# A new step plan, a new order of the setup and ten table columns on GpSimd, in a spectral-filter and maxout kernel

## The chip, the cores and the metric

The kernel runs on one core of one Trainium2 chip. The metric is the device time of one execution in microseconds (us). The span of a profiled execution is some 1.8 us shorter than the time that the device reports for it; spans are compared with spans, and times with times.

The profiled execution of the kernel before is not one of its two timed runs (528.76 and 528.07). It took 530.12 us with a span of 528.4, so that the span is only by chance equal to the median time of 528.41.

## The reference, cut to what matters

```python
B, seq, dim = 8, 3072, 256                     # 24,576 tokens
X = np.fft.rfft(x, axis=1)                     # along the sequence, per batch and channel
Y = X * (filt_r + 1j * filt_i)[None]           # one filter for all batches
y = np.fft.irfft(Y, n=3072, axis=1).astype(np.float32).reshape(24576, 256)
h1, h2 = y @ w1, y @ w2                        # 256 -> 1024
out = np.maximum(h1, h2) @ w_out               # 1024 -> 256
```

## The kernel before

The sequence of 3072 is split into 128 x 24, and each transform is done as two stages of matrix products with a product by the filter between them. The kernel uses max(h1, h2) = relu(h1 - h2) + h2, so the second half of the network needs one product with w1 - w2 (tile `ph`), a relu, and two products that add up in `po`.

The setup (the first 48 us) builds the sine tables, spreads the filter from the loaded rows over the partitions ("spreads", `expand_f`: products `pf`, copied into `F`), and sends batch 0 through all stages without a trip through memory (S1, T1, S2, S3, T2). Its order is written out by hand, since TensorE, ScalarE and VectorE take turns in it:

```python
    order = (1, 2, 3, 4, 5, 0, 6, 7)
    expand_f(1, 0, S)            # spread of group 1, real part, copied by ScalarE
    expand_f(2, 0, V)
    first_s1(0, S)
    expand_f(3, 0, V)
    sines_u(0)
    first_s1(1, S)
    # ... (cut: the rest, which the diff below shows)
    first_s1(5, S, 2)
    expand_f(6, 0, V)
    first_t1(1, V)
    first_t1(2, V)
    expand_f(1, 1, S)            # imaginary spreads from here on
```

After it comes the main loop: 48 output tiles of eight steps. In each step TensorE makes one `ph` of its own tile and two or three parts of `po` of the tile before. The transforms of the later batches are hung into steps by a plan:

```python
    def load_p(b, c):            # one x tile of batch b: two loads
        # ...
        for m in range(2):
            nc.sync.dma_start(out=xb[b, c][64 * m:64 * m + 64], in_=...)

    def fold_x(b, c):            # sums and differences of its halves, on Pool
        # ...
        for i, op in enumerate((OP.add, OP.subtract)):
            G.tensor_tensor(xb[b, c][:, i], xf[:, 0], xf[:, 1], op)

    def f1_read(b):              # eight reads of the first stage's result, from memory
        # ...
                    nc.sync.dma_start(out=bt[b][64 * blk:64 * blk + 48, t0:t0 + 8],
                                      in_=src[blk][:, e, 8 * h:8 * h + 8])

    def z_read(b, h):            # one read of half of the filtered spectrum
        # ...
        nc.sync.dma_start(out=zr[b][64 * h:64 * h + 64], in_=zd[b]...)

    def gen_f2(b):               # nine units: filter batch b, and first stage of b + 1
        # ...
        units = (2, 3, 4, 5, 6, 7) if b == 1 else (0, 1, 3, 4, 6, 7)
        for j, g in enumerate((4, 5, 6, 7, 2, 3, 1, 0)):
            if b + 1 < B and j in units:
                f1_half(b + 1, (3, 4, 5, 0, 1, 2)[units.index(j)] if b == 1 else units.index(j))
            # ... products px of bt, product with F on VectorE (pq), products pz of the group before,
            # ... copied by ScalarE (zt); every second group stores zd
            yield
```

```python
    def plan_x(n, steps, lag=12):
        for c, s_ in enumerate(steps):
            plan(s_, load_p, n, c)
            plan(s_ + lag, fold_x, n, c)
    # ...
    plan(5, f1_read, 1)
    plan_f2(1, spaced(15, 2.4, 9), 28, 36)      # nine units from step 15; z_read at 28 and 36
    # ... (cut: batch 2's x)
    plan(36, f1_read, 2)
    plan_x(3, spaced(24, 3, 6))                 # x of batch 3
    plan_f2(2, spaced(60, 2.5, 9), 74, 81)
    plan(83, f1_read, 3)
    plan_x(4, spaced(64, 3.5, 6))
    plan_f2(3, spaced(104, 3, 9), 121, 129)
    plan(130, f1_read, 4)
    plan_x(5, spaced(108, 3.5, 6))
    plan_f2(4, spaced(150, 3.3, 9), 168, 178)
```

The x loads, the reads of `bt` and `zr`, and the stores of `zd` are all issued by SyncE, one after the other. And from batch 2 on, the unit of F2(n) that comes first already needs a folded x tile of batch n + 1, because `f1_half(b + 1, ...)` is called ahead of `px`.

## Time and profile before

| | before |
|---|---|
| time, median of 2 runs | 528.41 us (528.07 to 528.76) |
| TensorE busy | 510.4 us, 97% of the span |
| start to first `ph` (the setup) | 48.2 us |
| first `ph` to the start of tile 7 (both stalls) | 78.3 us |
| half clock inside the loop | 3.41 us from 68.66 and 6.83 us from 113.03 |

The page, the waits and the table by stage are shown and read in the prediction. One more view is needed for the setup: VectorE's timeline just before its first copy of a spread (columns: start in us, busy us of the group, engine, line, operation, output and input, shape, number).

```profile
8.77 0.96 DVE L275 TENSOR_TENSOR uu<-uu 128x768 f32<-128x768 f32 x1
9.76 0.56 DVE L276 TENSOR_SCALAR uu<-uu 128x768 int32<-128x768 int32 x1
...
11.25 0.27 DVE L283 TENSOR_SCALAR uu<-uu,col 128x1 f32<-128x1 f32 x1
11.44 3.07 DVE L141 CAST F<-pf 128x512 bf16<-128x512 f32 x5
```

The cut lines are five of the ten column operations, 0.15 to 0.21 us each; they end at 11.2, and the operation on `ny` (L283) and the casts follow at once. VectorE is never idle here: what is taken off it ahead of the casts should bring them forward.

### The profile page before, as it was taken

To read this page: it belongs to the slowest core of one execution; us is meant where nothing else is said; L and a number is where in the kernel's file an instruction comes from. 1 tells how busy PE (TensorE), PEld (TensorE's weight loads), DVE (VectorE), ACT (ScalarE), POOL (GpSimd) and SP (SyncE) were. 2 spreads that over 40 slices of the span, in tenths; PEclk is the share of its full clock that TensorE was granted. 3 is DMA by queue.
4 is the path that set the end of the run, shared out by engine and by line. 5 is a ranking of instruction groups with operands and counts; after the bars stand their busy time and mean duration, and the time that the engine had idled before them with its cause. 6 is when DMAs were issued, how large, how long until landed. Compare 5 with 4: busy or idle time off the path is not lost.

```text
span 528.4 us, 12607 instructions
## 1 busy us (share of the span) xinstructions
PE 510.4 (97%) x5282; PEld 347.4 (66%) x5282; DVE 322.7 (61%) x438; ACT 336.6 (64%) x598; POOL 147.9 (28%) x168
## 2 busy tenths in 40 slices
PE   8999999969999999999999999999999999999997
PEld 3556656636667766676666666676766666677775
DVE  8987568423874476546784588546873588534442
ACT  7786659624886578856765576746775456545542
POOL 6684423352127302550055101830000000000000
PEclk9999989979999999999999999999999999999999
DMA  7994897989688979987898959996466935341212
GB/s 145 281 197 105 198 244 219 291 163 180 212 229 251 203 194 289 268 178 176 223 242 222 191 152 258 288 173 167 137 175 147 183 110 139 104 128 41 81 59 102
DMA packets 74093, 97.03 MB, mean 184 GB/s; under 512 B 5106, under 2 KB 49780, under 8 KB 73044
## 3 DMA queue, kind: packets, MB, share of 16 engines
q1 hardware_dynamic: 63012, 63.72, 53.5%
q0 software_dynamic: 11024, 32.51, 20.0%
q8 instruction: 41, 0.67, 0.6%
q14 instruction: 16, 0.13, 0.1%
HBM read 54.79 MB, written 47.19 MB: 193 GB/s over the span
## 4 chain that ended last, share of the span: by engine, by line
PE 86%; DMA 6%; DVE 3%; ACT 3%; issue 1%; SPq 0%; ACTq 0%
PE ph L610 31%; PE po L635 30%; PE po L630 7%; PE pz L447 4%; PE py L580 4%; DMA zd<-zt 3%; PE px L469 3%; PE pa L410 2%; DMA zr<-zd 1%; ACT F L514 1%; DMA bt<-ad 1%; PE pz L548 1%; DMA ad<-at 1%; PE pf L131 1%; PE pt L505 1%
## 5 line engine op out<-in xcount | busy, mean ns | idle before, releaser
L615 ACT ACTIVATE gt<-ph 128x512 bf16<-128x512 f32 x308 | 181.9, 602 | 127.2 <-PE ph L610 125.9
L635 PE MATMUL po<-Wo,gt 128*128 128x256 bf16 x1536 | 230.9, 273 | 0.0
L635 PEld LDWEIGHTS <-gt 128*128 128x128 bf16 x1536 | 150.8, 98 | 58.5 <-issue 1.0
L474 DVE TENSOR_TENSOR pq<-px,F 120x1024 bf16<-120x1024 f32 x112 | 131.8, 1219 | 30.8 <-PE px L469 30.5
L637 DVE COPY ot<-po 128x512 f32<-128x512 f32 x96 | 66.2, 690 | 104.8 <-PE po L635 104.5
L642 POOL DMA_DIRECT2D out_dram<-ot x47 | 25.7, 546 | 324.0 <-DVE ot L637 299.7
L402 POOL TENSOR_TENSOR xd<-xf 128x512 bf16<-128x512 f32 x72 | 89.1, 1267 | 38.8 <-DMA xf<-in_x_dram 30.9
L610 PEld LDWEIGHTS <-Wd 128*128 128x128 bf16 x768 | 71.0, 98 | 21.5 <-issue 13.0
L451 ACT ACTIVATE zt<-pz 112x512 bf16<-112x512 f32 x112 | 60.9, 601 | 18.7 <-PE pz L447 17.3
L613 DVE TENSOR_SCALAR gt<-ph 128x512 bf16<-128x512 f32 x76 | 52.2, 686 | 30.8 <-PE ph L610 24.9
L413 ACT ACTIVATE at<-pa 128x512 bf16<-128x512 f32 x72 | 39.1, 594 | 15.1 <-PE pa L410 14.5
L580 PE MATMUL py<-G,zr 128*128 128x128 bf16 x376 | 29.6, 221 | 5.2 <-DMA zr<-zd 4.7
L580 PEld LDWEIGHTS <-zr 128*128 128x128 bf16 x376 | 25.0, 99 | 8.0 <-issue 6.9
L447 PE MATMUL pz<-pq,VP 56*64 56x256 bf16 x448 | 28.8, 273 | 0.0
L447 PE MATMUL pz<-pq,VQ 56*64 56x256 bf16 x448 | 28.3, 271 | 0.0
L469 PE MATMUL px<-bt,U 48*64 48x256 bf16 x448 | 23.0, 276 | 1.8 <-DMA bt<-ad 1.8
L469 PEld LDWEIGHTS <-U 48*64 48x64 bf16 x448 | 11.6, 107 | 10.1 <-issue 5.4
L530 DVE TENSOR_TENSOR pq<-px,F 120x1024 bf16<-120x1024 f32 x11 | 13.2, 1221 | 3.5 <-ACT F L514 1.9
L447 PEld LDWEIGHTS <-VP 56*64 56x64 bf16 x448 | 13.6, 106 | 1.8 <-issue 1.7
L410 PE MATMUL pa<-xd,C 64*64 64x512 bf16 x144 | 14.8, 400 | 0.0
L514 ACT ACTIVATE F<-pf 128x1024 bf16<-128x1024 f32 x10 | 10.1, 1030 | 6.4 <-PE pf L134 6.4
L447 PEld LDWEIGHTS <-VQ 56*64 56x64 bf16 x448 | 13.4, 107 | 0.1
(389 smaller groups left out, 609.6 us busy)
## 6 DMA issues: line engine op xcount, KB each, us to landing
out_dram<-ot POOLq DMA_DIRECT2D x47, 512.0 KB, 5.0
xf<-in_x_dram SPq DMA_DIRECT2D x72, 256.0 KB
ad<-at SPq DMA_DIRECT2D x42, 256.0 KB
bt<-ad SPq DMA_DIRECT2D x56, 192.0 KB
zd<-zt SPq DMA_DIRECT2D x56, 192.0 KB
zr<-zd SPq DMA_DIRECT2D x14, 768.0 KB
xb<-in_x_dram POOLq DMA_DIRECT2D x12, 256.0 KB, 10.4
wf<-in_moe_w_dram POOLq DMA_DIRECT2D x2, 1024.0 KB, 10.4
```

Source lines behind the costliest of these rows:

```text
L402: G.tensor_tensor(xb[b, c][:, i], xf[:, 0], xf[:, 1], op)
L413: S.activation(at[:, 2 * m:2 * m + 2], pa[m], AF.Copy)
L447: TE.matmul(pz[c][64 * k:64 * k + 64, i], W[64 * c:64 * c + 56, 2 * g + i, k], pq[k][64 * c:64 * c + 56, ri, i], start=(ri == 0), stop=(ri ...
L451: S.activation(zt[0:ROWS, c, o:o + 2], pz[c][0:ROWS], AF.Copy)
L469: TE.matmul(px[k][64 * c:64 * c + 64, i], U[64 * k:64 * k + 48, 4 * g + 2 * i + c], bt_[64 * k:64 * k + 48, t_], start=True, stop=True)
L474: V.tensor_tensor(pq[k][0:FROWS], px[k][0:FROWS].rearrange("p (o i) d -> p o i d", o=1).to_broadcast([FROWS, 2, 2, D]), F[0:FROWS, :, k, 2 ...
L580: TE.matmul(py[:, n], zr[b][:, 4 * i + n, 128 * dc:128 * dc + 128], G1, start=True, stop=True)
L610: TE.matmul(ph, Wd[:, dc, 128 * j:128 * j + 128], y_[:, dc].rearrange("p a b -> p (a b)"), start=(dc == 0), stop=(dc == 1))
L613: V.tensor_scalar(gt[tt][:, j], ph, 0.0, None, OP.max)
L615: S.activation(gt[tt][:, j], ph, AF.Relu)
L635: TE.matmul(p_, g_[:, jj, 128 * n:128 * n + 128], Wo[:, jj], start=False, stop=(jj == 7))
L637: V.tensor_copy(ot[tt][:, n - 1:n + 1], po[tt])
```

## The change

Its intent: take away the two waits of TensorE for memory in batch 1 and 2, by moving units and by moving x loads out of the way of a store; start the first filter load earlier; take ten small operations off VectorE; and get the spreads, which unblock the first groups, ahead of S1.

```diff
+    load_f(0)                                   # ahead of three iotas
     tq = init.tile([128, 2, T], FP32)
 ...
-    load_f(0)
 ...
-    load_f(1)                                   # moved behind tables_u
 ...
-        V.tensor_scalar(mk[:, 0:1], ab, -TWO_PI, TWO_PI, OP.mult, OP.add)
-        V.tensor_tensor(mx, pb, ab, OP.add)
 ...                                             # ten such lines: V becomes G
+        G.tensor_scalar(mk[:, 0:1], ab, -TWO_PI, TWO_PI, OP.mult, OP.add)
+        G.tensor_tensor(mx, pb, ab, OP.add)
+        G.tensor_scalar(mk[:, 1:2], mx, TWO_PI, None, OP.mult)
+        G.tensor_scalar(mh, mk, 0.25, None, OP.mult)
+        G.tensor_scalar(mm, mk, -1.0, None, OP.mult)
+        G.tensor_scalar(t2, pn, 0.5, None, OP.mult)
+        G.tensor_scalar(na, t2, RND, RND, OP.add, OP.subtract)
+        G.tensor_tensor(t2, t2, na, OP.subtract)
+        G.tensor_scalar(t2, t2, t2, 2.0, OP.mult, OP.mult)
+        G.tensor_tensor(t2, t2, nb, OP.mult)
 ...
-        V.tensor_scalar(ny, ny, pb, t1, OP.mult, OP.add)
+        V.tensor_scalar(ny, ny, pb, t2, OP.mult, OP.add)
 ...
     expand_f(1, 0, S)
     expand_f(2, 0, V)
-    first_s1(0, S)
     expand_f(3, 0, V)
     sines_u(0)
-    first_s1(1, S)
+    first_s1(0, S)
     expand_f(4, 0, V)
     sines_u(1)
+    first_s1(1, S)
+    expand_f(5, 0, V)
     first_s1(2, S)
-    expand_f(5, 0, V)
+    expand_f(0, 0, V)
+    sines_u(2)
     first_s1(3, S)
-    sines_u(2)
-    expand_f(0, 0, V)
+    expand_f(6, 0, V)                           # real spread of group 6 during S1
     first_s1(4, V, 2)
 ...
     first_s1(5, S, 2)
-    expand_f(6, 0, V)
+    expand_f(1, 1, S)                           # imaginary spreads ahead of and around T1
     first_t1(1, V)
     first_t1(2, V)
-    expand_f(1, 1, S)
-    expand_f(7, 0, S)
+    expand_f(2, 1, S)
 ...                                             # spread 7 and the fix of F's first column: later;
                                                 # not shown: two copies of C1 on Pool, moved behind the tables
-    plan_f2(1, spaced(15, 2.4, 9), 28, 36)
+    plan_f2(1, spaced(17, 2.25, 9), 28, 36)
 ...
-    plan(36, f1_read, 2)
-    plan_x(3, spaced(24, 3, 6))
-    plan_f2(2, spaced(60, 2.5, 9), 74, 81)
-    plan(83, f1_read, 3)
-    plan_x(4, spaced(64, 3.5, 6))
+    plan(37, f1_read, 2)
+    plan_x(3, spaced(38, 3, 6))
+    plan_f2(2, spaced(58, 2.4, 9), 70, 78)
+    plan(80, f1_read, 3)
+    plan_x(4, spaced(83, 3, 6))
     plan_f2(3, spaced(104, 3, 9), 121, 129)
     plan(130, f1_read, 4)
-    plan_x(5, spaced(108, 3.5, 6))
+    plan_x(5, spaced(132, 3, 6))
     plan_f2(4, spaced(150, 3.3, 9), 168, 178)
```

More of the change, by code (lines that the diff above doesn't have):

```diff
@@ L233, in tables_u @@
         col = init.tile([128, 16], FP32)
-        pb, p6, pa_, pn, n2s, nb, ab, mx, na, t1 = [col[:, i:i + 1] for i in range(10)]
-        mk = col[:, 10:12]
-        mh = col[:, 12:14]
-        mm = col[:, 14:16]
+        pb, p6, pa_, pn, n2s, nb, ab, ah, t1 = [col[:, i:i + 1] for i in range(9)]
         m5 = init.tile([128, 2], FP32)
@@ L245, in tables_u @@
         V.tensor_tensor(ab, pa_, nb, OP.mult)
-        V.tensor_scalar(mk[:, 0:1], ab, -TWO_PI, TWO_PI, OP.mult, OP.add)
-        V.tensor_tensor(mx, pb, ab, OP.add)
-        V.tensor_scalar(mk[:, 1:2], mx, TWO_PI, None, OP.mult)
-        V.tensor_scalar(mh, mk, 0.25, None, OP.mult)
-        V.tensor_scalar(mm, mk, -1.0, None, OP.mult)
+        gc = init.tile([128, 10], FP32)
+        mk, mh, mm = gc[:, 0:2], gc[:, 2:4], gc[:, 4:6]
+        mx, t2, na = gc[:, 6:7], gc[:, 7:8], gc[:, 8:9]
+        G.tensor_scalar(mk[:, 0:1], ab, -TWO_PI, TWO_PI, OP.mult, OP.add)
[8 more added lines that the diff above has]
+        G.tensor_tensor(t2, t2, nb, OP.mult)
         V.tensor_scalar(m5[:, 0:1], pb, 0.5, None, OP.mult)
@@ L271, in tables_u @@
                             ub[:, dr].rearrange("p (o j) -> p o j", o=1).to_broadcast([128, T, J]), OP.add)
-        V.tensor_scalar(ab, ab, 0.25, None, OP.mult)
-        V.tensor_scalar(w[:, 0, 1], w[:, 0, 1], ab, None, OP.subtract)
+        V.tensor_scalar(ah, ab, 0.25, None, OP.mult)
+        V.tensor_scalar(w[:, 0, 1], w[:, 0, 1], ah, None, OP.subtract)
         V.tensor_scalar(a, w, RND, RND, OP.add, OP.subtract)
@@ L276, in tables_u @@
         V.tensor_scalar(a.bitcast(mybir.dt.int32), w.bitcast(mybir.dt.int32), 0x7FFFFFFF, None, OP.bitwise_and)
-        V.tensor_scalar(t1, pn, 0.5, None, OP.mult)
-        V.tensor_scalar(na, t1, RND, RND, OP.add, OP.subtract)
-        V.tensor_tensor(t1, t1, na, OP.subtract)
-        V.tensor_scalar(t1, t1, t1, 2.0, OP.mult, OP.mult)
-        V.tensor_tensor(t1, t1, nb, OP.mult)
         ny = a[:, 0, 0, 0:1]
-        V.tensor_scalar(ny, ny, pb, t1, OP.mult, OP.add)
+        V.tensor_scalar(ny, ny, pb, t2, OP.mult, OP.add)
         return uu, (mk, mh, mm), t1
@@ L652 @@
     table_c()
-    for e in range(2):
-        G.tensor_copy(C1.rearrange("p (e x u w) -> p e x u w", e=2, x=8, u=2)[:, e],
-                      Cz.rearrange("p (x u e w) -> p e x u w", x=8, u=2, e=2)[:, e])
     Zt = late.tile([128, 2, 128, N2], BF16, tag="l0", name="Zt")
@@ L662 @@
     uu, mk, t1 = tables_u()
-    done = []
+    load_f(1)
+    for e in range(2):
+        G.tensor_copy(C1.rearrange("p (e x u w) -> p e x u w", e=2, x=8, u=2)[:, e],
+                      Cz.rearrange("p (x u e w) -> p e x u w", x=8, u=2, e=2)[:, e])
     wf = load_w()
@@ L700 @@
             tables_pe()
-            expand_f(2, 1, S)
         if n < 6:
-            expand_f((0, 3, 4, 5, 6, 7)[n], 1, S)
+            expand_f((3, 4, 5, 0, 6, 7)[n], 1, S)
         if n < 2:
             load_x(1, 4 + n)
-        if n == 2:
-            fix_f()
         if n in (1, 3):
             tables_q(n // 2, S)
+        if n == 3:
+            fix_f()
+        if n == 4:
+            expand_f(7, 0, S)
         if n in (4, 6):
@@ L792, in in_f2 @@
     def in_f2(step):
-        return 0 <= step < 6 or 15 <= step < 36 or 60 <= step < 82 or 104 <= step < 130
+        return 0 <= step < 6 or 17 <= step < 36 or 58 <= step < 79 or 104 <= step < 130
     for tt in range(6 * B + 1):
```

## The prediction

> **What bounds the kernel now.** I began with the page's head: the busy shares, the 40-slice table and the chain that ended last.
>
> ```profile
> PE 510.4 (97%) x5282; PEld 347.4 (66%) x5282; DVE 322.7 (61%) x438; ACT 336.6 (64%) x598; POOL 147.9 (28%) x168
> PEclk9999989979999999999999999999999999999999
> PE 86%; DMA 6%; DVE 3%; ACT 3%; issue 1%; SPq 0%; ACTq 0%
> ```
>
> TensorE (PE) is the bound: 97% busy and 86% of the chain. But the chain also holds 6% of DMA, and the granted clock dips in slices 6 and 9, at about 66-79 and 106-119 us. PE therefore loses time in a few places. I asked the view of waits for PE alone, first from 66 us to the end and then from 120 us to the end; what the second still shows is the rest.
>
> ```profile
> PE py L580 <- DMA zr<-zd: 4.7, 1, 4.7
> PE px L469 <- DMA bt<-ad: 1.8, 2, 1.0
> ...
> PE ph L610 <- DVE pq L474: 0.7, 2, 0.3
> ```
>
> Columns: who waited for whom, us in total, times, longest. Past 120 us PE waits for 0.7 us in 408 us: what the new step plan does to batches 3 to 7 can win nothing there. The two DMA waits, at 65-67 and 110-115 us, are what the plan can win. The table by stage gives their price (columns: window, its length, busy us with instruction counts of PE, PEld, DVE, ACT, POOL, then granted clock, DMA share, GB/s).
>
> ```profile
> 60.00:65.00 5.00, 5.00 (x43) 3.59 (x41) 1.98 (x3) 2.88 (x5) 0.00 (x0) 1.00 0.84 133
> 65.00:70.00 5.00, 3.21 (x22) 1.77 (x22) 3.02 (x3) 1.17 (x3) 0.63 (x1) 0.87 1.25 158
> 70.00:75.00 5.00, 5.00 (x69) 3.01 (x67) 3.23 (x5) 2.80 (x7) 0.38 (x1) 0.79 1.09 267
> 110.00:115.00 5.00, 0.64 (x6) 0.33 (x4) 0.69 (x1) 0.60 (x1) 2.32 (x3) 0.80 1.01 198
> 115.00:120.00 5.00, 4.36 (x20) 2.51 (x21) 0.91 (x2) 1.20 (x2) 0.00 (x0) 0.51 1.28 160
> ```
>
> After each wait the clock falls to half: the raw clock records give 0.50 from 68.66 to 72.07 us (3.41 us) and from 113.03 to 119.86 us (6.83 us), and 1.00 in all the rest but the last 0.9 us. The chain in order of time says what the long wait was for:
>
> ```profile
> 92.02 9.81 DMA zd<-zt
> 101.83 0.02 issue
> 101.84 7.01 DMA zd<-zt
> 108.85 0.02 SPq L429
> 108.88 0.03 issue
> 108.91 6.34 DMA zr<-zd
> ```
>
> The last spectrum tiles of batch 1 left ScalarE at 98.5 us (timeline). The SyncE queue issued their store only at 100.23, because it stood 3.8 us in the issue of two x loads of batch 3; the store then took 7.0 us beside those loads, and the read back 6.3.
>
> **What the Trainium skill says.** "TensorE: Matmul & The Clock Gate", Part 1, gives a free-running activity window of 3413 ns after which an idle PE falls to half clock. The trace agrees: 3.41 and 6.83 us are one and two such windows. "DMA: Bandwidth & Descriptors", Issuing engines are not separate DMA queues, says that transfers of all issuing engines interleave on the same 16 engines. The trace agrees: stores zd of later batches with no load beside them go from issue to the issue of their read in 3.8-4.1 us (281.06 to 285.11, 340.13 to 344.13), against 7-10 us here. "SBUF — State Buffer", Who interferes with whom, says that VectorE in a two-port mode, or with two SBUF inputs, can block GpSimd; the trace before has no small Pool arithmetic in the table stage, so this is untested, and it counts as a risk for the ten moved columns.
>
> **Part 1, the step plan.** A step of the main loop without other work costs 0.98 us: eight steps from 102.66 to 110.5 us.
> - Start of F2(1), step 15 to 17. The first px starts at 64.95 and its last matmuls wait for bt until 67.34; step 16 begins at 67.57. A px alone costs 0.34 us, so the loss is 67.57-64.95-0.34 = 2.28 us. Two steps later it starts at 64.95+2x0.98 = 66.91 in the same frame and still waits about 0.3. Gain 1.95. The half clock then stretched 68.56 to 71.92 us (3.36 us) over work that costs 0.98+0.34+0.44 = 1.76 at full clock: 1.6 us, which goes too if the wait does. **Sum 3.5 us.**
> - The x loads of batch 3, steps 24-39 to 38-53: behind the read of zr. Call T0 the end of step 35, where the last zd tiles are now made (before: step 34). ScalarE empties them by T0+1.2; the store, free of loads, takes 4.05, so the read is issued at T0+5.3 and lands 6.3 later: T0+11.6. PE needs it after 12 steps and one s4: 12x0.98+0.45 = T0+12.2. The wait of 4.74 us should shrink to 0-0.5; I take 0.2. The half clock after it cost 2.0 us (116.66 to 120.39 for two steps worth 1.96, and 0.25 on py). **Sum 6.5 us.**
> - The denser units (2.25 steps apart, not 2.4; 2.4, not 2.5): ScalarE was without idle from 86.3 to 96.3 us, and with 14 relus of 0.56, six units of 2.18 and two y of 0.6 it needs 22.1 us for 14 steps in which PE needs about 21.8. **Cost 0.3 us.**
> - Will the later loads starve F2(2), now at step 58? They are issued behind bt(2), from about T0+14 on; the first lands near T0+18, is folded by T0+20.5, and step 58 is T0+23.5. Hidden, as are the moves of batches 4 and 5.
>
> **Part 2, the setup** (first 48.2 us, where PE waits little but PE, ScalarE and VectorE take turns).
> - The first filter load is issued ahead of three iotas of 0.37, 0.34 and 0.18 us: at 1.22, not 1.97. PE waits for it until 8.85, with its warm-up matmuls ending at 7.97. It and the six x tiles behind it (one each 1.25 us, DMA saturated) land 0.75 earlier.
> - Ten column operations of 0.15-0.21 us leave VectorE: 0.6 us ahead of the large table, 0.9 us behind it. VectorE's first cast, at 11.44, can start near 9.95 if Pool has its columns done by then.
> - VectorE gets the casts of group 6 (1.2 us) ahead of the last S1 copy, not behind it; ScalarE's chain of spreads, sines and S1 copies (9.51 to 18.72, nearly without idle) starts 0.75 earlier, but sines_u(2) now leaves a gap of some 0.7 us in it. T1 thus starts at 18.4-18.9, hardly earlier than 18.78. What wins is after it: two ScalarE copies of F (1.03 us each) fewer stand between the first groups. I reckon pq of group 2 at 24.3 (25.33 before) and of group 3 at 26.2 (27.65).
> - Later Pool gives some of it back: fix_f waits for F0's patch at 32.8, and spread 7 comes back on ScalarE at n=4. First ph at 47.4 instead of 48.2. **Gain 0.8 us.**
>
> **Sum:** 528.4 - 3.5 - 6.5 + 0.3 - 0.8 = 517.9; I put 518.0.
>
> **Rivals.**
> - *The zd store is hidden no better.* Its half of the plan moved one step later, and an output store of 512 KB still runs beside it. For: the read alone takes 6.3 us and leaves 0.6 us of slack. Against: the uncontended stores of 4.0 us. If the store takes 6 us, the wait is 1.5 us and may bring back the half clock: 520-521.
> - *ScalarE becomes the bound in the denser batch.* For: 10 us without idle at the old spacing. Against: those units still cost PE 1.10 us each, its own work. It would cost 1-2 us: 519-520.
> - *The setup gets slower.* Pool's ten columns wait on VectorE's port, and the tables end late. Against: they have 7.1 to 9.9 us for some 2 us of work. It would cost up to 1 us: 519-520.
> - *Everything is won*: both waits gone entirely and the setup ahead by 1.4: 516.
>
> **Range and chances.** The sum lies on the line of 2% (517.8), so the chances split. Errors point both ways: a full win gives 516, each rival alone 519-521. I give 515.6 to 521.2 eight times in ten; faster by over 2% 0.46, within 2% 0.53, slower 0.01.
>
> **What the profile after should show.** Clock 1.00 from start to end but for the last us; PE's wait for zr under 0.6 us and for bt under 0.5; a zd store of batch 1 in 4-5 us with no x load between it and the store before; the x loads of batch 3 in one run behind bt(2); first pf near 8.1 us, first VectorE cast near 10, T1 near 18.6, first ph near 47.4; the same PE busy time past 120 us. The prediction is wrong if a half-clock window stays, if PE waits for xd or bt at the start of F2(2), or if the setup's 0.8 us turns negative.

## The result

The changed kernel takes 534.50 us (median of 2 runs, 534.33 to 534.66) against 528.41. The ratio of after to before is 1.0115, with a 95% interval of 1.0071 to 1.0158. Here and below a ratio is the mean time of one kernel's fast runs over that of the other's of the same rounds, so it is not quite the ratio of the medians. 534.50 lies outside the predicted range of 515.6 to 521.2. The times differ by 6.1 us and the spans of the two profiled executions by 4.1, since the profiled one of before was slower than the timed ones.

The lines of the page of the kernel after that answer to those shown of before:

```profile
PE 507.1 (95%) x5204; PEld 348.1 (65%) x5282; DVE 321.9 (60%) x429; ACT 336.6 (63%) x597; POOL 151.9 (29%) x178
PEclk9999999999999999997999999999999999999999
PE 79%; DMA 7%; SPq 4%; DVE 3%; POOL 2%; issue 2%; ACT 2%; POOLq 0%; ACTq 0%
```

The page shows 3.3 us less of busy time on TensorE, but this is not a saving: the profile of after lacks 78 matmul records, 75 of them of `ph`, and shows 3.1 us of idle time without a cause ahead of `po` in their place (0.0 before). With these added it is 510.2 us against 510.4, in a span that is 4.1 us longer, so TensorE waited more. The two dips of the clock in slices 6 and 9 are gone, as intended. There is a new one in slice 19 (about 239 to 253 us), in a place where the kernel before had no wait at all. The chain has lost 7 points of TensorE and gained 4 of SPq, SyncE's sequencer. TensorE's waits past the setup (who waited for whom, us in total, times, longest):

```profile
PE pa L409 <- POOL xd L401: 6.4, 4, 2.9
PE ph L609 <- DVE pq L473: 0.9, 3, 0.3
PE px L468 <- DMA bt<-ad: 0.5, 1, 0.5
```

The wait for `zr` (4.7 us) is gone and that for `bt` fell from 1.8 to 0.5. In their place stands a wait for `xd`, an x tile folded by Pool: two of its four times in 118 to 136 us, where F2(2) starts, and two in 225 to 264 us, where F2(4) starts. The table by stage (columns as in the prediction) shows the place of the old stall and that of the new one:

```profile
110.00:115.00 5.00, 4.39 (x36) 3.00 (x34) 1.98 (x3) 2.16 (x5) 0.53 (x1) 1.00 1.26 163
115.00:120.00 5.00, 5.00 (x43) 3.68 (x41) 2.10 (x4) 2.97 (x5) 0.00 (x0) 1.00 1.17 246
...
240.00:245.00 5.00, 1.27 (x13) 0.63 (x13) 0.00 (x0) 0.46 (x1) 2.48 (x2) 0.89 1.06 306
245.00:250.00 5.00, 5.00 (x26) 2.50 (x20) 2.95 (x3) 2.28 (x4) 4.14 (x4) 0.50 1.07 233
```

At 110 to 120 us TensorE now works at full clock; before, it was busy for 0.64 us of the first five and then at a clock of 0.51. But at 240 to 245 us it is busy for 1.27 of 5 us, and the next five run at half clock: the raw record says 6.83 us of it.

What all of this is worth can be summed without a remainder, because every output tile has a first `ph`. The table below gives the length of seven stretches of the span, from the start of one tile to that of another, for both kernels and for the runs of the next section.

| run | setup, to tile 0 | tiles 0-6 | 7-11 | 12-17 | 18-19 | 20-46 | 47 and end | span |
|---|---|---|---|---|---|---|---|---|
| before | 48.2 | 78.3 | 50.5 | 59.1 | 21.1 | 255.1 | 16.0 | 528.4 |
| after | 50.3 | 69.4 | 54.2 | 59.1 | 28.1 | 255.1 | 16.3 | 532.5 |
| e1 plan only | 48.4 | 69.6 | 54.6 | 59.1 | 26.4 | 255.1 | 16.0 | 529.2 |
| e2 setup only | 50.3 | 75.4 | 50.8 | 59.1 | 21.1 | 255.1 | 16.3 | 528.1 |
| e3 x loads back | 50.3 | 78.5 | 51.0 | 61.4 | 21.1 | 255.1 | 16.3 | 533.7 |
| e4 x loads of 4, 5 back | 50.3 | 68.8 | 55.9 | 60.8 | 21.1 | 255.1 | 16.3 | 528.4 |
| e11 two x tiles first | 50.3 | 68.8 | 52.6 | 59.1 | 27.0 | 255.1 | 16.3 | 529.1 |
| e8 x of batch 3 split | 48.3 | 69.1 | 51.0 | 59.1 | 21.1 | 255.1 | 16.0 | 519.8 |
| e12 e8 and setup mended | 47.5 | 69.3 | 51.5 | 59.1 | 21.1 | 255.1 | 16.3 | 519.9 |

From before to after: setup +2.1, tiles 0-6 -8.9, tiles 7-11 +3.7, tiles 18-19 +7.0, end +0.3, rest 0; the sum is +4.2, and the spans differ by 4.1. The stalls of before were won almost as predicted, in this pair of executions; part of the 8.9 is half clock (10.24 us of it before, none here after), which differs from execution to execution. They came back later, and the setup lost.

**Where the new wait comes from.** SyncE's queue in the kernel after, from the last `zd` store of batch 1 on (start, time in issue, queue, operation, number):

```profile
99.13 1.05 SPq L455 DMA_DIRECT2D zd<-zt  x2
103.33 0.47 SPq L428 DMA_DIRECT2D zr<-zd  x1
103.91 8.46 SPq L422 DMA_DIRECT2D bt<-ad  x8
112.48 1.03 SPq L394 DMA_DIRECT2D xf<-in_x_dram  x1
```

The store now goes out at 99.13 and its read at 103.33, 4.2 us later (before: 100.23 and 108.9). That half of the plan works. Behind the read stand the eight reads of `bt`, which take SyncE 8.46 us, and only then the first x load of batch 3. What happened to that load is in the chain in order of time (start, us, what):

```profile
113.56 9.59 DMA xf<-in_x_dram
...
123.32 0.97 POOL xd L401
...
124.55 1.26 POOL xd L401
...
125.85 0.30 PE pa L409
```

The first x tile lands at 123.2, 10.7 us after the issue of its first half. In the transfers' own records the pieces of `bt`, 512 bytes each, go at some 300 per us (about 154 GB/s) until 119.5; x pieces appear only from about 119 on. Pool then needs 2.5 us for the two halves of the fold, and TensorE, which reached this unit at about 122.8, waits:

```profile
124.62 0.37 PE L409 MATMUL pa<-xd,C 64*64 64x512 bf16 x1 [1.84 <-POOL xd L401]
125.85 0.41 PE L409 MATMUL pa<-xd,C 64*64 64x512 bf16 x3 [0.85 <-POOL xd L401]
```

In brackets is the idle time before the instruction, and what ended it. F2(4) shows the same picture 120 us later: `bt` issued from 223.3, x from 230.85, the first fold at 241.95, and a wait of 2.88 us, which the clock then makes dearer. F2(3) shows no wait. The difference is in the plan: the read of `bt` and the first unit that needs the x loads behind it are 21 steps apart for F2(2) (37 to 58), 20 for F2(4) (130 to 150), and 24 for F2(3) (80 to 104).

**The setup.** VectorE's timeline in the kernel after, to be held against the one above:

```profile
8.16 0.96 DVE L279 TENSOR_TENSOR uu<-uu 128x768 f32<-128x768 f32 x1
9.15 0.56 DVE L280 TENSOR_SCALAR uu<-uu 128x768 int32<-128x768 int32 x1
11.76 0.27 DVE L282 TENSOR_SCALAR uu<-uu,col,gc 128x1 f32<-128x1 f32 x1 [2.05 <-POOL gc L254]
11.95 2.47 DVE L141 CAST F<-pf 128x512 bf16<-128x512 f32 x4
```

The table is ready 0.6 us earlier, as predicted, but VectorE then stands for 2.05 us until Pool has the last of its ten columns, and the first cast comes 0.5 us later than before instead of 1.5 earlier. Pool's timeline says why the columns took so long:

```profile
7.82 0.34 POOL L245 TENSOR_SCALAR gc<-col 128x1 f32<-128x1 f32 x1
8.25 0.92 POOL L246 TENSOR_TENSOR gc<-col 128x1 f32<-128x1 f32 x1
9.25 0.55 POOL L247 TENSOR_SCALAR gc<-gc 128x1 f32<-128x1 f32 x1
...
11.54 0.19 POOL L254 TENSOR_TENSOR gc<-gc,col 128x1 f32<-128x1 f32 x1
```

An operation on one element per partition takes Pool 0.19 us at 11.54, but 0.92 at 8.25, where it lies beside VectorE's subtraction (8.16 to 9.12), and 0.55 at 9.25, beside VectorE's bit mask (9.15 to 9.71). This agrees with "SBUF — State Buffer", Who interferes with whom, as cited in the prediction; it had been counted as a risk, and it came true. Together the ten took 3.9 us (7.82 to 11.73); on VectorE they had taken 0.15 to 0.21 us each.

Two more numbers locate the rest: from VectorE's first cast to T1 it is 9.67 us after and 7.34 before; from T1 to the first `ph` it is 28.65 after and 29.45 before. The new order loses 2.33 us ahead of T1 and wins 0.8 behind it.

### The profile page after: what moved, and what is told of

Read it like the earlier page. It is cut to its first block, busy times and chain, and to the rows that moved or that the text cites.

```text
span 532.5 us, 12542 instructions
## 1 busy us (share of the span) xinstructions
PE 507.1 (95%) x5204; PEld 348.1 (65%) x5282; DVE 321.9 (60%) x429; ACT 336.6 (63%) x597; POOL 151.9 (29%) x178
## 4 chain that ended last, share of the span: by engine, by line
PE 79%; DMA 7%; SPq 4%; DVE 3%; POOL 2%; issue 2%; ACT 2%; POOLq 0%; ACTq 0%
PE po L634 29%; PE ph L609 26%; PE po L629 7%; PE pz L446 5%; DMA xf<-in_x_dram 4%; SPq L422 3%; PE py L579 3%; PE px L468 3%; PE pa L409 2%; DMA zd<-zt 1%; DMA bt<-ad 1%; DVE pq L473 1%; POOL xd L401 1%; DMA ad<-at 1%; PE pz L547 1%
## 5 line engine op out<-in xcount | busy, mean ns | idle before, releaser
L401 POOL TENSOR_TENSOR xd<-xf 128x512 bf16<-128x512 f32 x72 | 89.2, 1268 | 41.4 <-DMA xf<-in_x_dram 36.8
L468 PE MATMUL px<-bt,U 48*64 48x256 bf16 x448 | 23.5, 276 | 0.5 <-DMA bt<-ad 0.5
L409 PEld LDWEIGHTS <-C 64*64 64x64 bf16 x144 | 4.5, 103 | 14.5 <-issue 13.0
```

What stands on the lines that cost most here:

```text
L468: TE.matmul(px[k][64 * c:64 * c + 64, i], U[64 * k:64 * k + 48, 4 * g + 2 * i + c], bt_[64 * k:64 * k + 48, t_], start=True, stop=True)
```

## The experiments

Where one run is given, the kernel was executed once, and its span can hold half clock by chance; such runs are read by their stretches and not by their time. The theory for the loop: the x loads stand behind the reads of `bt` in SyncE's one queue, and the first unit of F2(2) and of F2(4) needs them too soon. The rival: the denser units, or Pool, are the bound there. The theory for the setup: Pool's columns and the order of S1 and the spreads delay the first cast and T1. All kernels gave the right result except e15. Times in brackets are those of the kernel before on the same chip; it lay anywhere from 523.7 to 530.8 us, which is why spans and stretches carry the argument where no ratio is given.

**e1: the plan alone.** The kernel before, with the new step plan and the old setup.

```diff
 (setup as before)
-    plan_f2(1, spaced(15, 2.4, 9), 28, 36)   # and the seven lines below it
+    plan_f2(1, spaced(17, 2.25, 9), 28, 36)  # and the seven lines below it, as after
```

> The kernel before with the new step plan alone. Theory (the plan wins at the two DMA waits of batch 1 and loses at the starts of F2(2) and F2(4), the setup loses on its own): the first ph stays at 48.2 us as before; from first ph to tile 6 it takes 60.9 us, not 68.5; PE waits for folded x some 2.7 us near 120-125 us and 3.7 us near 240 us with a half clock after the second; span 532.5 - 2.1 = 530.4 us, so slower than before by 2 us. Rival (the setup's later loads upset the plan): the two waits for folded x are gone and the span falls to about 521.

Measured: 532.04 us (530.98 to 534.16, 4 runs) against 527.4 (7 runs), ratio 1.0086 [1.0034, 1.0137]. TensorE's waits past the setup begin with

```profile
PE pa L410 <- POOL xd L402: 5.0, 4, 2.5
```

The plan by itself is a loss: tiles 0-6 win 8.7 us, tiles 7-11 lose 4.1 and tiles 18-19 lose 5.3. The span of 529.2 is 1.2 shorter than expected.

**e2: the setup alone.** The setup of after, the plan of before.

```diff
+    (load order, Pool columns and order of the setup as after)
     plan_f2(1, spaced(15, 2.4, 9), 28, 36)   # plan as before
```

> The setup of after with the step plan of before. Theory: first ph at 50.3 us, 2.1 us later than before, the same two DMA waits as before (1.8 and 4.7 us), span 528.4 + 2.1 = 530.5 us. Rival (the setup moves only the phase and is made up later): first ph late but the span within 0.5 us of before.

Measured: 529.78 us (526.99 to 530.17) against 527.4, ratio 1.0026 [0.9975, 1.0078]; span 528.1. First `ph` at 50.3, as expected, 2.1 us later than before. But the span was not longer. TensorE's waits past the setup:

```profile
PE py L579 <- DMA zr<-zd: 3.1, 1, 3.1
PE px L468 <- DMA bt<-ad: 2.0, 2, 1.3
```

Both old waits are there, yet the clock fell to half for 3.41 us only, against 3.41 + 6.83 in the kernel before, and tiles 0-6 took 75.4 us instead of 78.3. The rival's forecast for the span came true, but this does not show that the shift of the setup saved the clock. Within one run the half-clock stretches begin on a raster of 3.41 us. Where this raster lies against the start of the program differs from run to run: the stretch from 68.66 us before lies 0.4 us past a multiple of 3.413, the one from 243.89 after 1.6, and the one from 115.90 here 3.3. The traces of all 17 runs, cut into the windows of their raster, show when the clock falls. All 27 falls from full clock (between 10 and 515 us) follow a window in which TensorE was busy for 55% or less. Of the 2,449 windows without a fall one alone was busy for less than 57% (50%, at 121 us after, in a profile that lacks records). How much half clock a wait brings thus depends on how the raster cuts it, and so in part on chance. By the times the setup costs 0.26%, with an interval from a gain to a loss, so its share in the whole is not settled by this run; but 1.0086 (e1) times 1.0026 is 1.0112, close to the 1.0115 of the whole change.

**e3: all x loads back.** The kernel after, with the x loads of batches 3, 4 and 5 at the old steps.

```diff
-    plan_x(3, spaced(38, 3, 6))
+    plan_x(3, spaced(24, 3, 6))
-    plan_x(4, spaced(83, 3, 6))
+    plan_x(4, spaced(64, 3.5, 6))
-    plan_x(5, spaced(132, 3, 6))
+    plan_x(5, spaced(108, 3.5, 6))
```

> After, with the x loads of batches 3, 4 and 5 planned at the steps of before; all else of after. Theory (the later loads are what starves F2(2) and F2(4)): PE's waits for folded x are 0, tiles 7 and 18 take 10 and 9 us, not 14.8 and 14.5; the wait for zr in batch 1 comes back in part (2 to 5 us). Span 532.5 - 4.6 - 7 + 2 to 7, so 523 to 528. Rival (the earlier or denser F2(2) starves on folds whatever the loads): waits for folded x stay above 2 us.

Measured: 536.01 us (533.05 to 537.59), ratio 1.0149 [1.0093, 1.0205]. The waits for `xd` are gone altogether, so the late loads are their cause and the denser units are not. In their place is

```profile
PE py L579 <- DMA zr<-zd: 7.1, 1, 7.1
```

with 10.24 us of half clock behind it: tiles 0-6 take 78.5 us, as long as before. So the expected 2 to 5 us of wait and the expected span of 523 to 528 were missed (the span was 533.7). The move of batch 3's loads is what wins the stall at `zr`, and it is what loses at F2(2). Neither of the two steps is right for all six tiles.

**e4: only the loads of batches 4 and 5 back.**

```diff
     plan_x(3, spaced(38, 3, 6))              # stays
-    plan_x(4, spaced(83, 3, 6))
+    plan_x(4, spaced(64, 3.5, 6))
-    plan_x(5, spaced(132, 3, 6))
+    plan_x(5, spaced(108, 3.5, 6))
```

> After, with the x loads of batches 4 and 5 alone at the steps of before, batch 3 late as in after. Theory: the 2.7 us wait for folded x near 123 us stays, the 3.7 us wait near 242 us and its half clock go: span 532.5 - 7 = 525.5. If the wait at F2(4) came from the shift of the whole schedule, it stays and the span is 532.

Measured: 529.57 us (527.96 to 530.76), ratio 1.0027 [0.9969, 1.0085]. The wait at F2(4) and its half clock are gone: tiles 18-19 take 21.1 us as before, 7.0 less than after. The wait at F2(2) stays (3.1 us). The span of 528.4 is 2.9 longer than expected: tiles 7-11 took 1.7 more than after, with 3.41 us of half clock among them, and a new wait cost another 1.7. This new one shows up at tile 13, in the timeline of VectorE:

```profile
191.51 0.69 DVE L636 COPY ot<-po 128x512 f32<-128x512 f32 x1 [4.12 <-DMA out_dram<-ot]
```

The plan of after has `f1_read(3)` at step 80 rather than 83, so that the last x tile of batch 4 landed behind it; Pool's fold of it waited until 185.12 (its halves landed at 184.3 to 184.5; the view names TensorE, which freed a buffer at 185.0, as the last to come), two output stores stood behind the fold in Pool's queue until 187.56, and VectorE had no free output buffer. The same disease, three links further on; it costs 1.7 us in tiles 12-17.

**e5: the ten columns back on VectorE.**

```diff
-        G.tensor_scalar(mk[:, 0:1], ab, -TWO_PI, TWO_PI, OP.mult, OP.add)   # and nine more
+        V.tensor_scalar(mk[:, 0:1], ab, -TWO_PI, TWO_PI, OP.mult, OP.add)   # in the old places
```

> After, with the ten column operations back on VectorE at their old places; all else of after. Theory (VectorE's wait of 2.05 us for the Pool columns is what delays the setup): that wait is gone, VectorE's first cast starts at about 11.3 us (11.95 in after), first ph at 49.0 to 49.6 us, against 50.3 in after and 48.2 before. Rival (the new order of spreads and sines is what delays it): first ph stays at 50.0 us or later.

Measured: one run of 532.45 us [526.91], span 530.6. First cast at 11.53 (after 11.95, before 11.44), first `ph` at 49.9. This lies between the theory (49.0 to 49.6) and the rival (50.0 or later), and both have a part: the columns cost 0.4 us, and the rest stays. The earlier filter load wins nothing that reaches the cast.

**e6: Pool keeps the columns, the five that VectorE waits for come first.**

```diff
         gc = init.tile([128, 10], FP32)
+        G.tensor_scalar(t2, pn, 0.5, None, OP.mult)        # the five t2 lines, moved up
+        # ...
         G.tensor_scalar(mk[:, 0:1], ab, -TWO_PI, TWO_PI, OP.mult, OP.add)
```

> After, with the same ten column operations on Pool, but the five that VectorE waits for first. Theory: VectorE's wait for Pool falls from 2.05 us to under 0.5, first cast near 10.3 us, first ph at 48.6 to 49.2 us. Rival (order of spreads and sines): first ph stays at 50.0 or later. If the Pool operation that runs beside VectorE's two-input subtract again takes about 0.9 us instead of 0.2, whichever of the ten it is, the length comes from the overlap and not from the operation.

Measured: one run of 534.53 us, span 532.8. VectorE's wait falls from 2.05 to 0.72 us, the first cast comes at 10.63, the first `ph` at 48.9. The operation that now lies beside VectorE's subtraction is of another kind, with one tensor input, and takes the same time:

```profile
8.29 0.92 POOL L246 TENSOR_SCALAR gc<-gc 128x1 f32<-128x1 f32 x1
```

So the 0.92 us belongs to what runs beside it, not to Pool's own speed at two inputs: the two-input operations elsewhere in this queue took 0.19 to 0.46 us. "GPSIMD Engine Reference", 4.1 Engine selection, says that Pool is about twice as slow as VectorE for two inputs and near line rate for one; on 128 single elements this trace shows no such split (0.19 to 0.27 us for both kinds where nothing lies beside them, against 0.15 to 0.21 on VectorE). The span gained nothing, for two half-clock windows of 3.41 and 6.83 us fell into the loop instead of one.

**e7: the old order of the setup, columns on Pool as after.**

```diff
     expand_f(2, 0, V)
+    first_s1(0, S)
     expand_f(3, 0, V)
     sines_u(0)
-    first_s1(0, S)
+    first_s1(1, S)                           # and so on: all lines of the order as before
```

> After, with the order of spreads, sines, S1 and the first groups of before (columns on Pool and load order as in after). Theory of the columns: VectorE still waits 2 us for them, first cast at 11.95 us and first ph 48.7 us or later (before had 11.44 and 48.2). Rival (the order costs the 2.1 us): first ph at 48.2 or earlier although VectorE waits.

Measured: one run of 532.19 us, span 530.0. First cast at 11.95, first `ph` at 48.8, T1 at 19.3. From the first cast to T1 it is 7.35 us again. With e6 this splits the loss of 2.1 us: 0.5 is the wait for Pool's columns, and 1.5 is the order.

**e8: another plan.** The setup of before; the units of after; but x of batch 3 in two halves: three tiles early, where SyncE is free, and used first, and three behind the reads of `bt`; x of batch 4 ahead of `f1_read(3)`, x of batch 5 as before.

```diff
-    plan_f2(1, spaced(15, 2.4, 9), 28, 36)
+    plan_f2(1, spaced(17, 2.25, 9), 28, 36)
-    plan(36, f1_read, 2)
-    plan_x(3, spaced(24, 3, 6))
+    for c, s_, f_ in ((3, 22, 34), (4, 24, 36), (5, 26, 38), (0, 38, 56), (1, 40, 58), (2, 42, 60)):
+        plan(s_, load_p, 3, c)
+        plan(f_, fold_x, 3, c)
+    plan(37, f1_read, 2)
-    plan_f2(2, spaced(60, 2.5, 9), 74, 81)
-    plan(83, f1_read, 3)
-    plan_x(4, spaced(64, 3.5, 6))
+    plan_f2(2, spaced(58, 2.4, 9), 70, 78)
+    plan_x(4, spaced(62, 2.8, 6))
+    plan(80, f1_read, 3)
-                f1_half(b + 1, (3, 4, 5, 0, 1, 2)[units.index(j)] if b == 1 else units.index(j))
+                f1_half(b + 1, (3, 4, 5, 0, 1, 2)[units.index(j)] if b < 3 else units.index(j))
```

> A version meant to beat both: the setup of before; F2(1) and F2(2) at the steps of after; the x loads of batch 3 split, three tiles whose buffers are free early at steps 22 to 26 and used first, three behind the read of bt(2); batch 4 ahead of f1_read(3), batch 5 as before. Theory: neither the wait for zr (under 1 us) nor for folded x (under 0.5 us), no half clock after 60 us but the last; first ph 48.2, tile 6 near 109.5 us, tile 8 near 129.5, span 528.4 - 7.4 = 521. Rival (any load near the stores of zd brings the wait back): wait for zr above 2 us, span 525 or more.

Measured: 522.61 us (521.51 to 522.94, 4 runs) against 526.91 (7 runs), ratio 0.9924 [0.9877, 0.9971]; span 519.8. The clock line of its page has no dip, and TensorE's longest waits past the setup are:

```profile
PE ph L610 <- DVE pq L474: 0.9, 3, 0.3
PE ph L610 <- ACT y__2169 L583: 0.5, 1, 0.5
...
PE px L469 <- DMA bt<-ad: 0.2, 1, 0.2
```

No wait for `zr` and none for `xd`. Tiles 0-6 take 69.1 us, tiles 18-19 take 21.1: what the change won is kept and nothing is paid back. Tiles 7-11 take 51.0 against 50.5 before. The units are as dense as after and the store of `zd` is as free; what differs is the place of the loads in the queue, with the order in which the tiles are used, and the old setup. By the times the gain is 0.76%, an estimated 4 us of 528, and not the 8.6 us between the two spans: the profiled run is the fastest of its four and is held against a slow one of before.

**e9: S1 ahead of the spreads, the rest as after.**

```diff
     expand_f(2, 0, V)
+    first_s1(0, S)
     expand_f(3, 0, V)                        # and so on up to spread 6; imaginary spreads as after
```

> After, with the S1 stages back ahead of the spreads that follow them (order of before up to T1, spread of group 6 behind S1 too); columns on Pool, imaginary spreads ahead of T1 and the rest as in after. Theory (in after each S1 stands on PE behind a spread that waits for VectorE's first casts, so PE and with it ScalarE's S1 copies are held up): first cast still at 11.95 us, PE's wait for VectorE's casts near 12 us falls from 1.8 to under 1 us, first ph at 48.8 us or up to 0.4 earlier, as with the whole old order. Rival (the imaginary spreads ahead of T1 and spread 7 in the loop cost it): first ph at 50.0 or later.

Measured: one run of 538.45 us, span 536.6, first `ph` at 51.7, a miss. T1 came 1.8 us earlier than after (19.84), but TensorE then waited 1.6 us in T1 for a copy of ScalarE, and 3.41 us of half clock fell into the setup at about 29 us. The first `ph` of this run says nothing of the order; e13 repeats the question.

**e10: only spread 6 back behind S1.**

```diff
-    expand_f(6, 0, V)
     first_s1(4, V, 2)
 ...
     first_s1(5, S, 2)
+    expand_f(6, 0, V)
```

> After, with the real spread of group 6 alone back behind S1. Theory as in the run before: T1 waits for ScalarE's last S1 copy, not for VectorE, so this gains little: first ph 49.7 to 50.3. Rival (the two casts of 1.2 us ahead of VectorE's S1 copy are what delays T1): first ph at 49.1 or earlier.

Measured: one run of 535.38 us, span 533.5; T1 at 21.08, first `ph` at 49.7. From the first cast to T1 it is 9.13 us. Spread 6 during S1 costs 0.54 of the 2.33 us.

**e11: two x tiles of batch 3 ahead of the reads of `bt`.** The queue theory by itself: nothing but the order of issue.

```diff
-    plan(37, f1_read, 2)
-    plan_x(3, spaced(38, 3, 6))
+    plan_x(3, [36, 36, 38, 41, 44, 47])
+    plan(37, f1_read, 2)
```

> After, with the first two x tiles of batch 3 issued ahead of the read of bt(2), the other four behind it; batches 4 and 5 as in after. Theory (one queue, first in first out: x waits until the 1.5 MB of bt in 512-byte pieces, some 10 us, are through): the first two folds no longer hold up PE near 123 us (wait for folded x there under 0.5 us) and bt comes 3 to 4 us later, so a wait for bt of at most 1.5 us takes its place; tile 7 takes 10 to 12 us, not 14.8. The untouched F2(4) keeps its wait of some 3.7 us near 240 us. Rival (Pool or the buffers hold up the folds): the wait near 123 us stays above 2 us.

Measured: one run of 530.92 us [529.46, 11 runs], span 529.1, 3.4 less than after. Tile 7 takes 11.7 us against 14.8 after, and what is left of the wait is F2(4)'s:

```profile
PE pa L409 <- POOL xd L401: 4.0, 2, 3.1
```

Two times, not four. The rival, that the denser units or Pool bound the start of F2(2), is out: the units and the folds are the same. Tiles 7-11 fell only from 54.2 to 52.6 us, since TensorE now waits 1.4 us at 138 us for a product of VectorE (`pq`) that stands ahead of a `py`.

**e12: e8's plan with a mended setup.** The old order, the early filter load, the columns on Pool with VectorE's five first.

```diff
+    (plan as in e8)
+    (load_f(0) ahead of the iotas; columns as in e6; order as before)
```

> The plan of e8 with a mended setup: order of spreads and S1 as before, first filter load ahead of the iotas, the ten columns on Pool with the five that VectorE waits for first. Theory: first cast near 10.6 us and, at the 36.85 us that the old order takes from first cast to first ph, first ph at 47.5 us; all else as e8, span 519.75 - 0.8 = 519.0, 1.2 to 1.8% faster than before. Rival (ScalarE or the x tiles bound the setup by then): first ph at 48.2, span 519.8.

Measured: 523.29 us (521.78 to 523.66, 6 runs) against 529.46 (11 runs), ratio 0.9897 [0.9866, 0.9929]; span 519.9. First cast at 10.62, first `ph` at 47.5, 0.8 earlier than e8. But the span, expected at 519.0, is the same as e8's, and the gain of 1.03% lies under the expected 1.2 to 1.8: tiles 0-6 take 0.2 us more, tiles 7-11 0.5, and the end 0.3. The loop of e8 sits closely behind its loads, and TensorE now waits 0.3 us for `zr` and 0.4 for `bt`. The two plans are the best and cannot be told apart: 1.0 per cent less than before in the one set of rounds, 0.8 in the other.

**e13: e9 again, with e6's columns.** One point was still open: which part of the new order costs the 1.5 us.

```diff
+    (columns as in e6)
     expand_f(2, 0, V)
+    first_s1(0, S)
     expand_f(3, 0, V)                        # and so on, as in e9
```

> Settles what in the new order of the setup costs the 1.5 us between VectorE's first cast and the first ph (38.3 us in the new order, 36.85 in the old). Here the kernel after has VectorE's five columns first on Pool (first cast 10.63, as in e6) and the S1 units ahead of the spreads as before; the imaginary spreads ahead of T1 and the late spread 7 stay as after. Theory, the interleaving of spreads and S1 ahead of T1 costs it (ScalarE waits 1.5 and 1.1 us ahead of two S1 copies): T1 near 18.6 and first ph near 47.6 to 48.1, 37.0 to 37.5 us after the first cast. Rival, it is what stands behind T1 (imaginary spreads, spread 7 late): T1 earlier, but first ph stays at 48.9, 38.3 us after the cast. If a half-clock window falls into the setup again, the number is void.

Measured: one run of 534.88 us [530.1], span 533.1. T1 at 18.68, as expected, 8.06 us after the first cast. The first `ph`, at 52.3, is void: 10.24 us of half clock fell into the setup, behind the same wait of 1.6 us in T1 as in e9.

**e14: only the imaginary spreads back behind T1.**

```diff
-    expand_f(1, 1, S)
     first_t1(1, V)
     first_t1(2, V)
-    expand_f(2, 1, S)
+    expand_f(1, 1, S)                        # the second one back behind tables_pe, that of group 0 first
```

> The kernel after with only the imaginary spreads of groups 1 and 2 back behind T1 and behind tables_pe, and that of group 0 ahead of 3, as before. Theory, the cost lies ahead of T1 in the S1 units: T1 stays at 21.6 or is at most 0.2 us earlier, and first ph stays at 50.3 within 0.4 us (38.3 us after the first cast). Rival, the imaginary spreads ahead of T1 cost it: first ph near 49.4, 37.4 us after the first cast.

Measured: one run of 534.33 us, span 532.1. First `ph` at 51.5, later than after; T1 at 22.21, since 3.41 us of half clock fell on the S1 units at about 15 us. From T1 to the first `ph` it is 29.32 us, against 28.65 after and 29.45 before. The rival (these spreads cost the 1.5 us) is out: they win 0.7.

**e15: only spread 7 and the fix of F's first column back.**

```diff
+    expand_f(7, 0, S)
     table_e(t1)
 ...
+        if n == 2:
+            fix_f()
-        if n == 3:
-            fix_f()
-        if n == 4:
-            expand_f(7, 0, S)
```

> The kernel after with only spread 7 back ahead of the first group and the fix of F's first column back at the third group, as before. Theory, the cost lies ahead of T1: first ph stays at 50.3 within 0.4 us, or gets later, since spread 7 then stands ahead of the first groups again. Rival, spread 7 at the fifth group costs 0.9 us late in the setup: first ph near 49.4.

Measured: a wrong result, by an error of the experiment: in this order the imaginary spread of group 0 comes at n = 3 and overwrites what the fix wrote at n = 2. Its first `ph`, at 55.7, with 6.83 us of half clock in the setup, is not used. T1 stayed at 21.60, which shows only that these lines do not reach T1.

Taken together, e7, e9, e10, e13 and e14 settle the place and the size of the loss. From the first cast to the first `ph` it is 38.3 us in each of the seven runs with the whole new order, and 36.8 to 37.0 in the five with the old one, so single runs will do here where no half clock falls in. The new order loses 2.33 us between the first cast and T1. With S1 ahead of the spreads again, and spread 6 behind it, 1.61 of this is gone (e13); spread 6 is 0.54 of that (e10), so the spreads 3, 4, 5 and 0 ahead of S1 units are about 1.1. That sum assumes that the parts add up; with e9 in place of e13 it is 1.78 that is gone. What is left is the imaginary spread of group 1. It is the only edit ahead of T1 in which e9 and e7 differ, both with the first cast at 11.95: in e7 T1 starts at 19.30, in e9 the products of this spread start at 19.29 and T1 follows at 19.84, 0.54 later (e13 against e12: 0.64). Behind T1 the new order wins 0.8, of which the imaginary spreads are 0.7 (e14). So having them ahead of T1 came out nearly even.

## Why the prediction was wrong

**The bound, and the two old stalls: right.** The prediction took TensorE as the bound, and both DMA waits for its loss, with the half clock as a part of the price. It gave 3.5 + 6.5 - 0.3 = 9.7 us for the loop up to F2(2). Tiles 0-6 won 8.9: tiles 0 to 2, where the first stall was, went from 32.5 to 29.6, 2.9 us, and tiles 3 to 6 from 45.8 to 39.8, 6.0 us. The terms were sized well for this pair of executions. But the 8.9 holds half clock, to which the prediction gave 1.6 + 2.0 = 3.6 us as if every execution had it, while 16 of the 26 other executions of before had a mean clock of 0.995 or more against 0.990. The store of `zd` took 4.2 us from issue to its read (4.05 predicted), the wait for `zr` was gone, and that for `bt` was 0.5 (0.3 predicted).

**The step that failed** is this one: "Will the later loads starve F2(2), now at step 58? They are issued behind bt(2), from about T0+14 on; the first lands near T0+18, is folded by T0+20.5, and step 58 is T0+23.5. Hidden, as are the moves of batches 4 and 5." T0, the end of step 35, was about 98 us (the last `zt` copies began at 98.03). The issue came at 112.48, as predicted. But the landing was put 4 us behind the issue, and it came 10.7 us behind it, at 123.2. The prediction does not say where the 4 us came from; it is what it had measured for stores with no load beside them. Here 1.5 MB of `bt` in pieces of 512 bytes stood ahead of it in the same rings, most of it still to come when SyncE had issued the last. An issue that is over says nothing of a transfer that is over. "DMA: Bandwidth & Descriptors", Queues, rings and completion order, says that SyncE owns one row of rings, and that on each DMA engine the descriptors of a ring are consumed in order; the trace agrees, with x pieces only from about 119 us and the pieces of `bt` ending at 119.5. The prediction cited the section on issuing engines for the sharing of the engines and left out the order within one queue. Yet its own case showed it: its slow store and the x loads beside it both went through SyncE, and in the trace before the 2048-byte pieces of x make up most of 101 to 104 us and the store's 512-byte pieces most of 104 to 106.

The second half of the same sentence, "as are the moves of batches 4 and 5", was not worked out at all. For batch 4 it held (24 steps from the read to the use), for batch 5 it did not (20 steps), and this was the dearer half: 7.0 us at F2(4), of which 3.7 is the wait and the rest is 6.83 us at half clock, an estimated 3.4 us. F2(2) cost 3.7 in tiles 7-11; of it, 2.7 is the wait. The reasoning "past 120 us PE waits for 0.7 us in 408 us: what the new step plan does to batches 3 to 7 can win nothing there" was true, and half of the thought. Where there is nothing to win, a plan that is moved can only lose, and each moved load has to be followed to its first user.

**The denser units: right.** They were given 0.3 us. In e8, with the same units and without the late loads, tiles 7-11 take 0.5 us more than before and tiles 0-6 9.2 less. ScalarE did not become the bound.

**The setup: wrong in sign.** It was given a gain of 0.8 and lost 2.1. Three of its terms can be told apart.
- "First pf near 8.1": it came at 8.67 (before 8.85). The first filter load was issued at 1.40 rather than 1.22, and the gain was 0.2 of the 0.75 us expected. Even that is inside the scatter: in the three runs with the old place of this load the first `pf` came at 8.85 to 9.38, in the other 14 at 8.47 to 9.47.
- "VectorE's first cast [...] can start near 9.95 if Pool has its columns done by then": Pool had not. The condition was written down, and dismissed in the rivals with "they have 7.1 to 9.9 us for some 2 us of work". The work began at 7.82, took 3.9 us, and was the last thing ready (11.73). With the right order of the ten (e6) the cast comes at 10.63; with them on VectorE, at 11.53 (e5).
- "T1 thus starts at 18.4-18.9": it started at 21.62. The prediction followed ScalarE's chain alone. The S1 units stand behind the spreads on TensorE, the spreads wait for VectorE's casts to free their banks, and so VectorE's late start and its casts stand ahead of ScalarE's copies; in the trace ScalarE sat idle for 1.48 us ahead of one S1 copy and for 1.12 ahead of another. What the prediction said of the time behind T1, a gain of some 0.8 us by the imaginary spreads, is what was measured: 0.8, of which e14 gives 0.7 to them. It left out that the one of group 1, now ahead of T1, delays T1 by 0.54 (e9 against e7).

**The rivals.** That the setup gets slower was named, by the right mechanism for the columns, and sized at up to 1 us; the columns were 0.5 of it, and the order, which it did not name, 1.5. That `zd` is hidden no better, and that ScalarE becomes the bound, were both wrong. The last sentence of the prediction lists "if PE waits for xd or bt at the start of F2(2)" and "if a half-clock window stays" among what would make it wrong: both are what happened, though they had been given nothing in the sum or in the range. With F2(2) at 3.7, F2(4) at 7.0 and the setup at 2.9 short of its mark, 13.6 of the 14.6 us between the predicted 517.9 and the span of 532.5 are accounted for; 0.8 is what the old stalls gave less than predicted, and 0.3 is the end, so that the terms sum to 14.7.

**What would still have been missing.** The late loads are not the whole of it. The sum starts from 528.4, the span of the slow execution, and is read as a time. In e8 and e12 both stalls are won and nothing is paid back, and they still took 522.6 and 523.3 us, above the upper end of the range (521.2); their ratios, put on 528.41, give an estimated 524.4 and 523.0. So the forecast gain of 10.5 us was about twice what a plan without the late loads brings in time, and the half clock of one execution, priced as a sure gain, is the likely reason; no run tests that by itself.

## What to carry to other kernels

When a load is moved out of the way of one transfer, follow it to its first user, and count what stands ahead of it in the same queue as transfers, not as issues: what was issued last here landed last, and 1.5 MB in small pieces took some 10 us. Splitting a group of loads in two, one half ahead of the obstacle and used first and one half behind it, kept the whole gain here where either place alone lost it. Small operations that are handed to an idle engine win only if their results come back before the first engine needs them: put the ones it waits for first, and look at what runs beside them. Before the half clock of one profile is priced as a gain, see how many executions of the same kernel have it.

## What the Trainium skill lacked or had wrong

- "TensorE: Matmul & The Clock Gate", the table under Why this matters for your kernels, advises against idle gaps of TensorE of over about 3 us. Here shorter gaps cost clock too, and equal ones do not always: two waits of 1.8 us in all, the longest 1.0, left a window of the raster 48% busy and brought 3.41 us of half clock (before, 68.66 us), while two of 1.84 and 0.85 fell into two windows, 50% and 69% busy, and brought none (after, F2(2)). What is lacking is the busy share of a window at which the clock falls: in the 17 traces 27 falls came after 0 to 55%, and one alone of 2,449 windows without a fall was under 57%.
- "DMA: Bandwidth & Descriptors", Queues, rings and completion order, has the order within a ring but no figure for what it costs a load that stands behind others: here an x load whose issue began right behind eight reads of `bt` (1.5 MB in 512-byte pieces, some 300 pieces per us) landed 10.7 us later, while the issue of those reads itself had taken 8.46 us.
- No page gives the fixed cost of so small an operation on Pool: here seven of them in a row, with VectorE idle beside them, took 1.8 us (after, 9.89 to 11.73), 0.19 to 0.27 us each. On the interference of VectorE with Pool the runs have nothing to correct.
